# Attention and feed-forward on one core: the first step's v is loaded through ScalarE's DMA queue instead of SyncE's

## The chip, the cores and the metric

The kernel runs on one core of a Trainium2 chip. The metric is the device time of one execution in microseconds (us). Engines are named as in the profile: PE is TensorE (PEld its weight loads), DVE is VectorE, ACT is ScalarE, POOL is GpSimd, SP is SyncE. A DMA is issued by an instruction in the stream of an engine (here SP or ACT), which puts it into that engine's DMA queue; the bytes are moved by 16 DMA engines, which both queues share.

## What is computed

Sigmoid attention over 8 batches with 12 heads of 448 tokens and a head dimension of 64, and then a feed-forward layer with a squared ReLU over the 3584 tokens:

```python
scores = scale * np.matmul(q, k.transpose(0, 1, 3, 2)) - np.log(S)
attn = 1.0 / (1.0 + np.exp(-scores))
x = np.matmul(attn, v)            # then tokens x 768
h = x @ w_in
r = np.maximum(h, 0.0)
out = (s * (r * r) + b) @ w_out
```

The attention weights need no sum over the keys, so a block of scores can be used as soon as its sigmoid is there.

## The kernel before, in words

The attention part is a row of 24 steps, three for each of the 8 batches. One step works on four heads, as two pairs (index `i`); the two heads of a pair lie in the upper and the lower 64 partitions. A step's queries and keys stand in one tile `qk` (128 partitions, pair, queries or keys, 448 tokens: 896 KB), its values in a tile `v` (448 KB). After the 24 steps the feed-forward part runs to the end of the kernel (lines 556 to 1251); it isn't touched.

The fp32 products are made of three products of split numbers: a high part `qkh` and a low part `qkl` of queries and keys, and the products high by high, high by low and low by high (`PARTS`). For most steps ACT makes the high part and DVE the low part; for the first two steps DVE makes both, in pieces (`parts_dve`, lines 390 to 396, called in lines 594 and 601).

One step does this on PE: the scores of six key blocks of 128 tokens (`scores`, L420; the first two blocks of the first step use the unsplit numbers, L426, so that they needn't wait for a split), ACT's sigmoid on each block (L400), then the product with v (`attn_v`, L454, tile `pav`), and the remaining 64 keys of both pairs (`scores_last`, L441, and `attn_v_last`, L463). In the first step the products with v of the first pair come right behind its scores; the last keys' scores of this step follow, and then the second pair's products.

The order of the instructions on each engine is the order in which the program writes them. The tiles' semaphores are set by a framework; each engine works off its own list in order. A tile that several engines use is waited for by its readers.

The beginning of the program, around the change, is this:

- The first step's `qk` comes in five DMAs (`load` with `first=True`, lines 358 to 368): SP issues the first 128 keys of the first pair (L361), the rest of its keys (L363) and the second pair's keys (L365); ACT issues the first pair's queries (L362) and the second pair's queries (L364).
- `load_v` (lines 370 to 373) loads a step's v, and `load` without `first` the whole `qk` of a step in one DMA (L367); both are issued by SP.
- After these, ACT loads its table and computes a sigmoid into `e_bias` (L476), and DVE overwrites `e_bias` with a constant (L477). This stands ahead of DVE's first split.
- PE runs eight matmuls on constants (`WARM`, L482) before its first scores.
- SP then issues the first two pieces of the weights (L503, `st`), the second step's v and two small vectors (L549, L550).

DVE's first splits come in the order of line 594: the first pair's queries (448 columns), the second pair's queries, a block of the first pair's keys (128 columns), and the second pair's keys (384 columns).

```python
    loaded = {0: load(*quads[0], first=True)}
    load_v(*quads[0], loaded[0])
    loaded[1] = load(*quads[1])
    nc.scalar.activation(e_bias, nls, AF.Sigmoid)
    nc.vector.memset(e_bias, -896.0 * 2.0**23)
```

Of the kernel before, what the change touches and what calls it, by code (L numbers as in the profile page):

```python
# [94 lines left out]
def sigmoid_attention_relu2_ffn(  # L95
# [10 lines left out]
    nc = tc.nc  # L106
# [248 lines left out]
    quads = [(b, t) for b in range(B) for t in range(NQ)]  # L355
    NL = len(quads)

    def load(b, t, first=False):
        x = ld.tile([P, 2, 2, S], F32, tag="qk", name=f"qk_{b}_{t}")
        if first:  # L360
            nc.sync.dma_start(x[:, 0, 1, :P], qk[b, t][:, 0, 1, :P])  # L361
            nc.scalar.dma_start(x[:, 0, 0], qk[b, t][:, 0, 0])  # L362
            nc.sync.dma_start(x[:, 0, 1, P:], qk[b, t][:, 0, 1, P:])  # L363
            nc.scalar.dma_start(x[:, 1, 0], qk[b, t][:, 1, 0])  # L364
            nc.sync.dma_start(x[:, 1, 1], qk[b, t][:, 1, 1])  # L365
        else:
            nc.sync.dma_start(x, qk[b, t])  # L367
        return [x]

    def load_v(b, t, ld_):  # L370
        vt = ldv.tile([P, 7, 2, D], F32, tag="v", name=f"v_{b}_{t}")
        nc.sync.dma_start(vt, v[b, t])
        ld_.append(vt)

    NX = S + 3 * P
# [95 lines left out]
        nc.sync.dma_start(x_dram[b][:, 2 * t : 2 * t + 2], o)  # L471

    loaded = {0: load(*quads[0], first=True)}
    load_v(*quads[0], loaded[0])
    loaded[1] = load(*quads[1])
    nc.scalar.activation(e_bias, nls, AF.Sigmoid)  # L476
    nc.vector.memset(e_bias, -896.0 * 2.0**23)  # L477
# [68 lines left out]

    ticks(-1, "SP")
    load_v(*quads[1], loaded[1])
    nc.sync.dma_start(s_sb, s)  # L549
    nc.sync.dma_start(b_sb, b_)  # L550
# [44 lines left out]
    for n, (b, t) in enumerate(quads):  # L595
# [35 lines left out]
        if n + 2 < NL:  # L631
            load_v(*quads[n + 2], loaded[n + 2])
# [657 lines left out]
```

## Time and profile before

| | |
|---|---|
| time, median of 3 runs | 1038.63 us (1038.63 to 1038.81) |
| the profiled execution's own time | 1039.04 us |
| its span | 1037.2 us |
| PE busy | 1033.5 us (100% of the span) |
| DVE busy | 837.3 us (81%) |
| ACT busy | 617.0 us (59%) |
| DMA, mean over the span | 277 GB/s |
| granted TensorE clock | 1.00 |

The profile is of one execution. The page gives for each engine its busy time and share, and the chain of work that ended last, followed back from the last instruction. The timeline gives the start of an instruction, its length, the engine, the line, what it writes and reads, and in brackets how long the engine had been idle before it and what ended that. An engine's name with a q (SPq, ACTq) stands for the issue of a DMA or for a wait in its instruction stream; when the bytes have landed is given by the DMA view, as the time from the issue's start to the landing. Matmul ends are modelled, so the sum of PE's busy time isn't the time in which it works at its peak.

### The profile page before, as it was taken

What the parts mean: (1) busy time and instruction counts of PE and PEld (TensorE: products, weight loads), DVE (VectorE), ACT (ScalarE), POOL (GpSimd) and SP (SyncE); (2) the same over time, 40 slices, a digit from 0 to 9 for tenths busy, and PEclk for the clock granted to TensorE, in tenths of its full rate; (3) what the DMA queues carried; (4) which work ended last, traced back from release to release, by engine and by line L of the source; (5) the groups of instructions that cost most, each with busy time, mean ns of one, the idle gap of its engine ahead of it and who ended that gap; (6) DMA issues with size and microseconds to landing.
All of it is one profiled execution on the core that took longest, in us unless ns stands there. A gap on an engine that the chain in (4) does not pass through costs nothing.

```text
span 1037.2 us, 13906 instructions
## 1 busy us (share of the span) xinstructions
PE 1033.5 (100%) x5290; PEld 780.9 (75%) x5290; DVE 837.3 (81%) x910; ACT 617.0 (59%) x666; POOL 0.2 (0%) x4
## 2 busy tenths in 40 slices
PE   9999999999999999999999999999999999999998
PEld 4545555555888888888888888888888888888887
DVE  5999999995988965898898897796455789888777
ACT  7999999988776755564445344344445335552432
POOL 0000000000000000000000000000000000000000
PEclk9999999999999999999999999999999999999999
DMA  9788989994999999999686676897666666676773
GB/s 334 265 333 340 359 321 393 345 398 190 338 362 366 358 409 410 340 341 322 201 267 190 218 230 219 292 317 249 197 192 194 194 192 196 191 233 212 221 227 119
DMA packets 101569, 287.17 MB, mean 277 GB/s; under 512 B 10240, under 2 KB 20352, under 8 KB 101504
## 3 DMA queue, kind: packets, MB, share of 16 engines
q1 hardware_dynamic: 101216, 285.84, 79.3%
q8 instruction: 42, 0.69, 0.3%
q10 hardware_dynamic: 288, 0.46, 0.1%
q14 instruction: 23, 0.19, 0.0%
HBM read 198.18 MB, written 88.08 MB: 276 GB/s over the span
## 4 chain that ended last, share of the span: by engine, by line
PE 100%; DVE 0%; issue 0%
PE o L1225 31%; PE h L1095 31%; PE pav L454 11%; PE psc L420 9%; PE ph L563 6%; PE po L765 6%; PE psc_l L441 2%; PE pav L463 2%; PE idle L482 0%; PE psc L426 0%; DVE C_t L181 0%
## 5 line engine op out<-in xcount | busy, mean ns | idle before, releaser
L1095 PE MATMUL h<-s_0h,wu 128*128 128x512 f32 x480 | 148.0, 389 | 0.0
L1095 PE MATMUL h<-s_1h,wu 128*128 128x512 f32 x480 | 147.8, 389 | 0.0
L400 ACT ACTIVATE a<-psc,nls 128x896 f32<-128x896 f32 x144 | 132.7, 1008 | 12.9 <-PE psc L420 10.1
L454 PE MATMUL pav<-a,v 128*64 128x448 f32 x576 | 113.8, 543 | 0.0
L1095 PEld LDWEIGHTS h<-s_0h,wu 128*128 128x128 f32 x480 | 90.1, 188 | 18.8
L1095 PEld LDWEIGHTS h<-s_1h,wu 128*128 128x128 f32 x480 | 90.1, 188 | 18.6
L968 ACT COPY G<-h 128x1024 f32<-128x1024 f32 x48 | 48.8, 1017 | 85.4 <-PE h L1095 57.7
L860 ACT ACTIVATE G<-G,b_sb,s_sb 128x1024 f32<-128x1024 f32 x48 | 59.8, 1246 | 61.4 <-DVE G L857 60.7
L1095 PE MATMUL h<-s_0l,wu 128*128 128x512 f32 x240 | 93.4, 389 | 0.0
L1095 PE MATMUL h<-s_1l,wu 128*128 128x512 f32 x240 | 93.4, 389 | 0.0
L454 PEld LDWEIGHTS pav<-a,v 128*64 128x64 f32 x576 | 39.1, 137 | 63.8 <-issue 45.4
L178 DVE TENSOR_TENSOR G<-G,h 128x1024 f32<-128x1024 f32 x40 | 48.8, 1219 | 39.1 <-PE h L1095 38.9
L1225 PE MATMUL o<-g_3h,wu 128*128 128x512 f32 (+1 forms) x244 | 79.0, 385 | 0.0
L1225 PE MATMUL o<-g_1h,wu 128*128 128x512 f32 x240 | 78.8, 389 | 0.0
L1225 PE MATMUL o<-g_2h,wu 128*128 128x512 f32 x240 | 78.8, 389 | 0.0
L1225 PE MATMUL o<-g_0h,wu 128*128 128x512 f32 x240 | 78.8, 389 | 0.0
L765 PE MATMUL po<-g,w 128*128 128x512 f32 x288 | 67.7, 389 | 0.0
L765 PEld LDWEIGHTS po<-g,w 128*128 128x128 f32 x288 | 54.1, 188 | 11.2
L563 PE MATMUL ph<-x0h,w 128*128 128x512 f32 x192 | 61.7, 390 | 0.0
L420 PE MATMUL psc<-qkh 64*128 64x448 f32 x284 | 54.8, 382 | 0.0
L1225 PEld LDWEIGHTS o<-g_3h,wu 128*128 128x128 f32 x244 | 45.6, 188 | 9.2
L1225 PEld LDWEIGHTS o<-g_0h,wu 128*128 128x128 f32 x240 | 45.1, 188 | 9.4
(152 smaller groups left out, 2029.7 us busy)
## 6 DMA issues: line engine op xcount, KB each, us to landing
wu<-wd SPq DMA_DIRECT2D x240, 512.0 KB, 3.8
wd<-t SPq DMA_DIRECT2D x36, 768.0 KB, 8.1
qk<-qk_t SPq DMA_DIRECT2D x23, 896.0 KB, 7.1
st<-w_out SPq DMA_DIRECT2D x16, 768.0 KB, 9.3
st<-w_in SPq DMA_DIRECT2D x16, 768.0 KB, 9.2
wd<-w SPq DMA_DIRECT2D x16, 768.0 KB, 5.9
v<-v_t SPq DMA_DIRECT2D x24, 448.0 KB, 5.4
xd<-xo SPq DMA_DIRECT2D x24, 448.0 KB, 4.4
```

The source lines that it names most:

```text
L178: nc.vector.tensor_tensor(o, x, y, op=ALU.add)
L400: nc.scalar.activation(a, psc[:, :, :S], AF.Sigmoid, bias=nls, scale=SCALE)
L420: nc.tensor.matmul(o[:, j, :S], two[wi][r, i, cols], two[xi][r, i, :S], start=m == 0, stop=m == 2,)
L441: nc.tensor.matmul(psc[half[i], j, :S], x[r, i, 1, 3 * P :], x[r, i, 0, :], start=True, stop=True,)
L454: nc.tensor.matmul(pav[r, i, :S], ld_[1][:, 3 * i + c, j, :], a[i, c][:, j, :], start=c == 0, stop=False,)
L463: nc.tensor.matmul(pav[r, i, :S], ld_[1][half[i], 6, j, :], a[half[i], j, :], start=False, stop=True,)
L563: nc.tensor.matmul(ph, w[:, k, wi, kc * P : (kc + 1) * P], x0[h][xi][:, cc, :], start=m == 0, stop=m == 3 * NCC - 1,)
L765: nc.tensor.matmul(pos[e], w[:, k, wi, kc * P : (kc + 1) * P], g[:, gi, :], start=first and i == 0, stop=last and i == 2,)
L860: nc.scalar.activation(x, x, AF.Identity, bias=b_sb, scale=s_sb)
L968: nc.scalar.copy(g(m, h), bk)
L1095: nc.tensor.matmul(bk[:, j], wt[:, j, wi, c * P : (c + 1) * P], opd[i][xi][:, c, :], start=i == ch[0] and m == 0, stop=m == 3 * KC - 1, sk ...
L1225: nc.tensor.matmul(o, wt[:, f, wi, e * P : (e + 1) * P], g[gi][:, f, tk], start=(end or i == ch[0] and p == 0) and f == 0 and m == 0, stop ...
```

## The change

The first step's v is issued by ACT, after the second pair's queries, and no longer by SP, between the second pair's keys and the second step's `qk`. All other loads of v are issued by SP as before.

```diff
-    def load_v(b, t, ld_):
+    def load_v(b, t, ld_, queue=None):
         vt = ldv.tile([P, 7, 2, D], F32, tag="v", name=f"v_{b}_{t}")
-        nc.sync.dma_start(vt, v[b, t])
+        (queue or nc.sync).dma_start(vt, v[b, t])
         ld_.append(vt)
...
     loaded = {0: load(*quads[0], first=True)}
-    load_v(*quads[0], loaded[0])
+    load_v(*quads[0], loaded[0], nc.scalar)
     loaded[1] = load(*quads[1])
```

On ACT, at the start of the program (`qk_0_154` is the first step's tile of queries and keys, `v_0_160` its values), the difference is:

```order
 L362 DMA qk_0_154<-qk_t 128x448
 L364 DMA qk_0_154<-qk_t 128x448
+L372 DMA v_0_160<-v_t 128x896
 L476 ACT_TABLE_LOAD
 L476 ACTIVATE e_bias<-nls 128x1 [waits DVE_49]
```

One DMA has come in, ahead of the table load and the activation.

On SP, at the same place (`qk_1_162` is the second step's tile of queries and keys, `st_0_175` the first piece of the weights), it is:

```order
 L363 DMA qk_0_154<-qk_t 128x320
 L365 DMA qk_0_154<-qk_t 128x448
-L372 DMA v_0_160<-v_t 128x896
 L367 DMA qk_1_162<-qk_t 128x1792
 L503 DMA st_0_175<-w_out 128x768
```

The same DMA has gone, and the second step's queries and keys follow the second pair's keys directly. The rows that follow on SP are the same as before; the second piece of the weights, next but one, waits for the semaphore of the first pair's queries. On PE, DVE and POOL no instruction has moved and no wait has changed.

## Prediction

> **What bounds the kernel now.** I read the page first: the busy shares and the chain of work that ended last.
>
> ```profile
> span 1037.2 us, 13906 instructions
> PE 1033.5 (100%) x5290; PEld 780.9 (75%) x5290; DVE 837.3 (81%) x910; ACT 617.0 (59%) x666; POOL 0.2 (0%) x4
> PE 100%; DVE 0%; issue 0%
> ```
>
> TensorE (PE) is busy for 1033.5 of 1037.2 us and the chain consists of its work alone. A load can therefore move the time only by opening or closing a hole in PE. The change touches the first microseconds, so I read the chain there next, with the window 0 to 26 us (columns: start, length, what).
>
> ```profile
> 0.77 3.15 PE idle L482 x8
> 3.92 2.98 PE psc L426 x8
> 6.90 2.43 PE psc L420 x24
> 9.33 2.41 PE pav L454 x12
> 11.74 0.91 PE psc_l L441 x8
> ```
>
> The pieces join without a gap: 0.77 + 3.15 = 3.92, 3.92 + 2.98 = 6.90, and so on. PE begins with eight warm-up matmuls (L482), and from then on nothing is waited for. So the kernel before has nothing that an earlier v could give back: v is needed by pav (L454), at about 9.3, and pav follows on the heels of the scores. What can happen is that some load now comes later than PE has room for. So the working is a list of loads, each with its landing and the time at which PE would notice.
>
> The landings come from the DMA view, one window for each issue (KB each, us from issue to landing). In this order they are: the first pair's queries, the second pair's queries, the second pair's keys, the first step's v, and the next step's queries and keys.
>
> ```profile
> qk<-qk_t ACTq DMA_DIRECT2D x1, 224.0 KB, 2.8
> ...
> qk<-qk_t ACTq DMA_DIRECT2D x1, 224.0 KB, 3.6
> qk<-qk_t SPq DMA_DIRECT2D x1, 224.0 KB, 4.1
> ...
> v<-v_t SPq DMA_DIRECT2D x1, 448.0 KB, 5.3
> ...
> qk<-qk_t SPq DMA_DIRECT2D x1, 896.0 KB, 7.1
> ```
>
> Their issue times, and all who use the data, stand in the timeline:
>
> ```profile
> 0.72 0.41 ACTq L362 DMA_DIRECT2D qk<-qk_t  x1
> 1.16 0.45 ACTq L364 DMA_DIRECT2D qk<-qk_t  x1
> 1.64 0.42 SPq L365 DMA_DIRECT2D qk<-qk_t  x1
> 1.65 1.28 ACT L476 ACT_TABLE_LOAD   x1 [1.65 <-PEq L1280]
> 2.10 0.43 SPq L372 DMA_DIRECT2D v<-v_t  x1
> 2.58 0.43 SPq L367 DMA_DIRECT2D qk<-qk_t  x1
> 2.94 0.20 ACT L476 ACTIVATE e_bias<-nls 128x1 f32<-128x1 f32 x1
> 3.05 1.12 SPq L503 DMA_DIRECT2D st<-w_out  x2
> 3.21 0.06 DVE L477 MEMSET e_bias<- 128x1 f32 x1 [2.35 <-ACT e_bias L476]
> 3.58 0.40 DVE L394 CAST qkh<-qk 128x448 fp32r<-128x448 f32 x1 [0.32 <-DMA qk<-qk_t]
> 4.82 0.40 DVE L394 CAST qkh<-qk 128x448 fp32r<-128x448 f32 x1 [0.18 <-DMA qk<-qk_t]
> 5.76 1.01 ACT L400 ACTIVATE a<-psc,nls 128x896 f32<-128x896 f32 x1 [2.62 <-PE psc L426]
> 6.25 0.35 DVE L394 CAST qkh<-qk 128x384 fp32r<-128x384 f32 x1
> 6.64 0.56 DVE L181 TENSOR_TENSOR qkl<-qk,qkh 128x384 fp32r<-128x384 f32 x1
> 7.14 0.19 PEld L420 LDWEIGHTS psc<-qkh 64*128 64x128 f32 x2
> 7.54 0.20 PEld L420 LDWEIGHTS psc<-qkh,qkl 64*128 64x128 f32 x2
> 9.26 0.20 PEld L454 LDWEIGHTS pav<-a,v 128*64 128x64 f32 x4 [0.31 <-issue]
> 9.77 0.59 DVE L394 CAST qkh<-qk 128x832 fp32r<-128x832 f32 x1 [2.58 <-DMA qk<-qk_t]
> 11.96 1.03 DVE L181 TENSOR_TENSOR qkl<-qk,qkh 128x832 fp32r<-128x832 f32 x1
> 14.99 0.98 PE L441 MATMUL psc_l<-qk 64*64 64x448 f32 x8
> 16.65 0.47 PE L420 MATMUL psc<-qkh 64*128 64x448 f32 x2
> ```
>
> Issue plus delay gives the landings: second queries 1.16 + 3.6 = 4.76, second keys 1.64 + 4.1 = 5.74, v 2.10 + 5.3 = 7.40, next step's pair of tensors 2.58 + 7.1 = 9.68.
>
> **The change, part by part.**
>
> *One issue less on SyncE (SP).* SP loses an issue of 0.43 us (0.48 to the next one), and the next step's queries and keys go out at 2.10 instead of 2.58. At best they land 0.48 earlier, at 9.2. VectorE (DVE) waited 2.58 us for them before 9.77 and would end their split about half a microsecond sooner than 11.96 + 1.03 = 12.99. PE first touches this tensor at 14.99 and its split parts at 16.65, so there were already 2.0 us or more of room: worth 0. The later SP issues keep their places, because the second weight piece behind them waits for the landing of the first queries (0.72 + 2.8 = 3.52), which nothing here moves.
>
> *One issue more on ScalarE (ACT).* The issue stands between the second queries and the table load, and takes about what it took on SP, 0.43 us (ACT's own two took 0.41 and 0.45), with some 0.04 between neighbours: 0.47. The table load moves from 1.65 to 2.12 and the activation on e_bias from 2.94 to 3.41, ending at 3.61. Behind it waits DVE's memset of e_bias (L477), and behind that, in DVE's order, the whole first split. The memset moves from 3.21 to 3.68, so the first cast starts at about 3.75 instead of 3.58: 0.17 late. DVE then sat idle for 0.18 us before the cast at 4.82, waiting for the second queries. This hides the 0.17, with next to nothing left over; 0 on the path. If the cover were gone the 0.17 would reach the keys' split, where there is 0.34 more (next paragraph). ACT's own next work, the sigmoid at 5.76, had been preceded by 2.62 us of idling: 0.
>
> *The bytes of v in another queue.* This is the open term. Before, the second keys and v shared SP's queue, keys first, v behind them. Now v stands behind the second queries in ACT's queue and is not held behind the keys: from the moment that the second queries have been sent, somewhat before they land at 4.76, v's packets mix with the keys' packets. The keys can land later. I take the room for this from the rows: DVE reached the second keys at 6.25, 6.25 - 5.74 = 0.51 after they landed. Their low part was ready at 6.64 + 0.56 = 7.20, and PE loaded it as weights at 7.54: another 0.34. (The high part, ready at 6.25 + 0.35 = 6.60 and loaded at 7.14, has 0.54.) So the keys may land up to 0.51 + 0.34 = 0.85 later, at 6.59, before PE stops; each further microsecond is a microsecond of the kernel, since PE has no later slack.
>
> How late will they be? One bound is no delay, 5.74. The other is that keys and v change places entirely, and the keys land where v landed, at 7.40: 7.40 - 6.59 = 0.81 us lost. What lies between depends on how fast bytes flow while both are under way, and the windows of half a microsecond show a dip just there (last columns: DMA share, GB/s):
>
> ```profile
> 4.00:4.50 0.50, 0.50 (x2) 0.35 (x4) 0.49 (x1) 0.00 (x0) 0.00 (x0) 1.00 1.01 382
> 4.50:5.00 0.50, 0.50 (x4) 0.24 (x2) 0.32 (x2) 0.00 (x0) 0.00 (x0) 1.00 1.68 283
> 5.00:5.50 0.50, 0.50 (x2) 0.10 (x2) 0.47 (x2) 0.00 (x0) 0.00 (x0) 1.00 0.51 179
> ```
>
> From 4.5 to 5.5 the rate averages 231 GB/s, against 382 just before; the engines are taken all the same (a share of 1.68 and 0.51, about 1.1 on average). Long packets begin there, at the point where v's turn comes. If v's first packets are slow by themselves, they will now be slow in front of keys that have not been sent. The earlier sharing of the two queues is seen from 3.4 to 3.7:
>
> ```profile
> q10 hardware_dynamic: 39, 0.07, 60.1%
> q1 hardware_dynamic: 39, 0.04, 41.3%
> ```
>
> Both queues sent 39 packets in that time: they are served packet by packet in turn. [...]
>
> With even turns the keys' 224 KB share the engines with 224 KB of v or, v's packets being twice as large (3.5 KB for a partition against 1.75 KB), with up to 448 KB of it. At 382 GB/s that adds 224/382 = 0.6 to 448/382 = 1.2 us to a full overlap; if a third of the keys is through before it begins (they are issued 0.48 after the second queries, and land 0.98 after them), it is 0.4 to 0.8 us: the keys land at 6.1 to 6.5, just inside 6.59. I take 0.1 us for this term, near the lower end, and keep 0 and 0.81 as its bounds.
>
> *v itself.* It is needed by the first pav, 9.26, and landed at 7.40: 1.86 us of room. It is issued 0.48 earlier (about 1.62), and starts about when it started before, now sharing with the keys and then with the next step's tensor. I count 0; its lateness is the rival below.
>
> Sum: 0 + 0 + 0.1 + 0 = 0.1 us. The profiled execution took 1039.04 us, 1.84 more than its span; it becomes 1039.1. The median of the runs shown is 1038.63, 0.41 below the profiled one, so I forecast 1038.7.
>
> **Rivals.**
>
> *The keys are passed by v* (the upper bound). PE waits at the second pair's scores, at about 7.54, for up to 0.81 us. For it speaks the dip after 4.5; against it the equal packet counts. Time: 1038.63 + 0.3 to 0.8, so 1038.9 to 1039.4.
>
> *v comes too late, and the kernel is slower.* The place is the first pav (9.26). In SP's queue the next step's tensor goes out in packets of 7 KB for a partition, twice v's, and those of the weight pieces behind it are nearly as large, so v may get a third of the rate or less. The deciding point is a landing after 9.26. If v finishes only together with the next step's tensor, at 9.68, PE loses 9.68 - 9.26 = 0.42. If ACT's queue were starved until the weight pieces behind that tensor had landed too, it would be much more: their two issues end at 3.05 + 1.12 = 4.17, the second begins about 0.6 before that, and it landed 9.7 later,
>
> ```profile
> st<-w_out SPq DMA_DIRECT2D x1, 768.0 KB, 9.7
> ```
>
> so at about 13.3, and PE would lose 13.3 - 9.26 = 4.0 us, the kernel taking 1042.7. Over 0.2% (2.1 us) needs a landing of v after 11.3. Against it stand the equal counts of packets above: ACT's queue was not starved.
>
> *Nothing at all moves* (the change does not do what it says for the queues: bytes flow through the same sixteen engines, v lands where it did). Then 1038.63, as good as the forecast. A gain would need a hole in PE to close, and the chain shows none after 0.77; I allow 0.1 us for scatter.
>
> **How the numbers follow.** About 0.2% (2 us) is what a measurement of this kernel can tell from no change. Chances: the forecast, with the keys late but inside or nearly inside the room (nothing moving included), 0.62; keys passed by v, 0.28; v too late 0.07, of which 0.04 for more than 2.1 us; a gain of whatever kind 0.03, of which 0.01 over 0.2%. The likeliest is 1038.7. The range reaches from 1038.2 (0.4 below the median, about the distance between the runs shown and the profiled one, the other way) to 1039.5 (the upper bound of the keys, 1039.4, and 0.1 of scatter). Faster by over 0.2%: 0.01; slower by over 0.2%: 0.04; within: 0.95.
>
> **What would show it.** After the change the chain must still be PE alone, with warm-ups, raw scores, split scores and pav joined without gaps; pav's first piece at 9.33, or up to 0.8 later if the keys are passed. The table load should start near 2.12, the memset of e_bias near 3.7, the first cast near 3.75, and the cast at 4.82 should stay. The second keys should land at 6.1 to 6.5, and the cast at 6.25 start on time or wait for a DMA; v should land between 7 and 9, and the next step's tensor between 9.2 and 9.7. The forecast is wrong if the first pav waits for v, if PE's weight loads at 7.1 to 7.6 wait long for DVE, or if the time differs by more than 1 us while this first stretch has not moved.

## The result, and the profile after

| | before | after |
|---|---|---|
| median of 19 runs | 1038.89 us | 1040.72 us |
| lowest and highest | 1038.62 to 1039.5 | 1038.64 to 1043.21 |
| ratio, 95% interval | | 1.0018 (1.0012 to 1.0024) |
| profiled execution, its span | 1039.04, 1037.2 | 1040.07, 1038.1 |

The change costs 1.83 us, or 0.18%. It also makes the kernel scatter: 0.9 us lay between the extremes before, 4.6 us lie between them now, and the best execution after is as fast as the best before. The profiled execution is one of the milder ones, 1.03 us over the profiled one of before. Its page has PE at the same busy time in a longer span, and the chain has a DMA in it that wasn't there:

```profile
span 1038.1 us, 13906 instructions
PE 1033.4 (100%) x5290; PEld 780.4 (75%) x5290; DVE 837.3 (81%) x910; ACT 616.9 (59%) x666; POOL 0.2 (0%) x4
PE 99%; DMA 1%; ACTq 0%; DVE 0%; issue 0%
```

The chain in the window 0 to 26 us of the kernel after shows which:

```profile
1.18 0.45 ACTq L364
1.62 0.03 issue
1.66 8.23 DMA v<-v_t
9.88 0.14 issue
10.02 2.48 PE pav L454 x12
12.49 0.91 PE psc_l L441 x8
```

pav begins at 10.02 where it began at 9.33, and behind it everything follows without a gap as before. The start of the kernel is now bound by v itself, which lands at 9.88. In the timeline after, the instructions that answer to those of before are these:

```profile
1.66 0.45 ACTq L372 DMA_DIRECT2D v<-v_t  x1
2.11 0.43 SPq L367 DMA_DIRECT2D qk<-qk_t  x1
2.14 1.28 ACT L476 ACT_TABLE_LOAD   x1 [2.14 <-issue]
3.70 0.06 DVE L477 MEMSET e_bias<- 128x1 f32 x1 [2.84 <-ACT e_bias L476]
3.71 0.39 DVE L394 CAST qkh<-qk 128x448 fp32r<-128x448 f32 x1
4.68 0.39 DVE L394 CAST qkh<-qk 128x448 fp32r<-128x448 f32 x1
6.92 0.36 DVE L394 CAST qkh<-qk 128x384 fp32r<-128x384 f32 x1 [0.73 <-DMA qk<-qk_t]
7.43 0.47 PE L420 MATMUL psc<-qkh 64*128 64x448 f32 x2 [0.52 <-DVE qkh L394]
10.02 2.48 PE L454 MATMUL pav<-a,v 128*64 128x448 f32 x12 [0.39 <-DMA v<-v_t]
```

There are two holes in PE. At 7.43 it waits 0.52 us for the high part of the second pair's keys, which DVE could only begin at 6.92 because the keys landed late; at 10.02 it waits 0.39 us for v. The holes sum to 0.91. The matmuls before the first hole ran a little earlier than before (the eight of L426 took 2.46 us in the timeline instead of 3.06), so pav's start moves by less, 0.69 in the chain (9.33 to 10.02), and the span ends 0.9 later. The DMA view of the same execution (v, second keys) gives the delays:

```profile
v<-v_t ACTq DMA_DIRECT2D x1, 448.0 KB, 8.2
qk<-qk_t SPq DMA_DIRECT2D x1, 224.0 KB, 5.3
```

v takes 8.2 us instead of 5.3, though it was issued 0.44 earlier; the keys take 5.3 instead of 4.1 and land at 1.64 + 5.3 = 6.94 (6.90 by the report of their last engine). What v's bytes do is seen by the packets of ACT's queue (q10) in three windows, 4.5 to 6.5, 6.5 to 8 and 8 to 9.2 (packets, MB, share of the engines):

```profile
q10 hardware_dynamic: 119, 0.38, 50.7%
...
q10 hardware_dynamic: 14, 0.05, 7.6%
...
q10 hardware_dynamic: 7, 0.02, 3.7%
```

Most of v is through by 6.5. What comes later is a handful of packets, and they set the landing. The trace has sixteen reports of v's landing, read here as one from each of the 16 DMA engines for its own share; their times are:

```
v after:   5.99 6.01 6.07 6.17 6.38 6.39 6.43 6.45 6.46 6.47 6.49 6.63 6.87 8.46 9.29 9.88
v before:  6.20 6.25 6.29 6.39 6.49 6.60 6.66 6.83 6.84 6.99 7.04 7.08 7.28 7.34 7.39 7.45
```

Thirteen engines finished earlier than the latest of before, and three were up to 2.4 us later than that. On the late ones v's last packets stand about 0.41 us apart (7.12, 7.52, 7.92, 8.33, 8.73, 9.14): 140 ns for a packet of v and 272 ns, the length of one of the second step's 7 KB rows, between two of them. Before, in one queue, v's last engine (7.45) reported ahead of the first one of the second step's tensor (8.68). pav began only behind the last of the sixteen: at 10.02, 0.14 us after 9.88.

### The profile page after: what moved, and what is told of

Read it like the earlier page. It is cut to its first block, busy times and chain, and to the rows that moved or that the text cites. A ratio compares the mean times of both kernels' runs of the same rounds, so it can differ in the third digit from the quotient of the medians.

```text
span 1038.1 us, 13906 instructions
## 1 busy us (share of the span) xinstructions
PE 1033.4 (100%) x5290; PEld 780.4 (75%) x5290; DVE 837.3 (81%) x910; ACT 616.9 (59%) x666; POOL 0.2 (0%) x4
## 4 chain that ended last, share of the span: by engine, by line
PE 99%; DMA 1%; ACTq 0%; DVE 0%; issue 0%
PE o L1225 31%; PE h L1095 31%; PE pav L454 11%; PE psc L420 9%; PE ph L563 6%; PE po L765 6%; PE psc_l L441 2%; PE pav L463 2%; DMA v<-v_t 1%; ACTq L364 0%; DVE C_t L181 0%; ACTq L362 0%
## 5 line engine op out<-in xcount | busy, mean ns | idle before, releaser
L420 PE MATMUL psc<-qkh 64*128 64x448 f32 x284 | 54.7, 382 | 0.5 <-DVE qkh L394 0.5
L1225 PEld LDWEIGHTS o<-g_2h,wu 128*128 128x128 f32 x240 | 45.1, 188 | 9.4
```

What stands on the lines that cost most here:

```text
L420: nc.tensor.matmul(o[:, j, :S], two[wi][r, i, cols], two[xi][r, i, :S], start=m == 0, stop=m == 2,)
L1225: nc.tensor.matmul(o, wt[:, f, wi, e * P : (e + 1) * P], g[gi][:, f, tk], start=(end or i == ch[0] and p == 0) and f == 0 and m == 0, stop ...
```

## The experiments

Three theories were set against each other: that v takes turns with SP's loads, so that the last engines of v and of the keys come late ("turns"), that a load issued by ACT is slow by itself ("ACT queue"), and that the later table load and what hangs on it cost the time ("ACT shift"). "Before" in the results is the kernel before, run on the same chip: a median of 1038.82 us for e1 to e4, 1038.91 for f1 to f3 and g1, and a single run of 1039.56 for h1 to h3. The ratio is that to this median, with its 95% interval.

### SP's later loads held back (e1_hold)

The second step's load stands behind DVE's second piece of the first split; the column that DVE writes is overwritten by the load. For this the first step's splits are written earlier in the program.

```diff
+        if hold:
+            nc.vector.memset(x[:, 1, 1, S - 1 :], 0.0)
...
+    def next_load():
+        loaded[1] = load(*quads[1], hold=True)
```

> The kernel after the change, with all of SP's loads from the second step's queries and keys onward held back until DVE has split the second pair's queries (about 5.9 us; DVE writes one column of that tile first, so that the load has to wait for it). v stays on ACT. Theory 'turns' (v, no longer ahead of SP's loads, takes turns with them on every DMA engine): with nothing on SP behind the keys, v lands by 7.2 and pav does not wait for it; 1038.7 to 1039.4. Theory 'ACT queue' (a load issued by ACT is slow or late by itself): v lands at 8 to 11 as after the change, 1040 to 1041.5. Theory 'ACT shift' (the later table load and the later second keys cost the time): 1040 or more, with pav on time and the holes in the scores.

Measured: 1040.3 (1039.03 to 1040.99), ratio 1.0013 (1.0004 to 1.0022). The profiled execution was the fastest, with keys at 6.2, v at 6.8 and no hole; the median was far from it. So a loss is there without the later loads, which "turns" as I had put it did not say. Where it arises this profile doesn't show, hence two more executions.

### The same kernel in two more executions (h1_hold, h2_hold)

> The kernel of e1_hold (v on ACT, SP's later loads held) once more for its profile, since its first profile was its fastest execution (1039.03) while its median was 1040.3. 'Turns': in an execution over 1039.8 the second pair's keys, which share the engines with v alone, land at 7.4 or later, and the hole is at the second pair's scores; v lands by 7.5 and pav does not wait for it.

> As h1_hold, a second look. If an execution over 1039.8 has its keys by 6.7 and v by 8, the loss lies elsewhere, most likely behind the hold itself (the second step's tensor and the weights come some 4 us later), and e1_hold says nothing on the keys.

Measured: 1040.44 and 1040.52, 0.9 and 1.0 over the single run of before. The timeline of h1_hold, and below it that of h2_hold, at the second pair's keys:

```profile
7.54 0.36 DVE L396 CAST qkh<-qk 128x384 fp32r<-128x384 f32 x1 [1.37 <-DMA qk<-qk_t]
8.05 0.47 PE L424 MATMUL psc<-qkh 64*128 64x448 f32 x2 [1.03 <-DVE qkh L396]
```

```profile
7.78 0.36 DVE L396 CAST qkh<-qk 128x384 fp32r<-128x384 f32 x1 [1.62 <-DMA qk<-qk_t]
8.29 0.47 PE L424 MATMUL psc<-qkh 64*128 64x448 f32 x2 [1.52 <-DVE qkh L396]
```

The keys land at 7.52 and 7.76, v at 7.70 and 7.93, and pav waits for nothing. With v alone beside them the keys land up to two microseconds later than in the profile of before, and a hole of 1.0 and 1.5 us opens at the scores. The packets show the turns: in h2_hold the last packets of the keys begin at 6.39, 6.60, 6.81, 7.01 and 7.22, some 0.21 us apart, which is one packet of keys (74 ns) and one of v (140 ns). That is "turns", with the keys as its victim.

### v back on SP, the second step's tensor on ACT (e2_swap)

```diff
-    loaded[1] = load(*quads[1])
+    loaded[1] = load(*quads[1], queue=nc.scalar)
```

> The kernel before the change, with the second step's queries and keys issued by ACT in the place where the change puts v; v is on SP as before, directly behind the second pair's keys. 'Turns': v again takes turns, with the 896 KB now on ACT; it lands at 8 to 11, pav waits, 1039.3 to 1041.5. 'ACT queue': v is on SP and lands by 7.6; 1038.6 to 1039.2. 'ACT shift': ACT has one issue more, as after the change; 1040 or more with v on time.

Measured: 1041.66 (1041.12 to 1043.59), ratio 1.0029 (1.0017 to 1.0040), so at least as bad as the change, with v on SP (its median excess is larger, but the two intervals overlap). "ACT queue" is out: v is late (2.10 + 8.2 = 10.3) from SP's queue too. The place that I had named was wrong, since pav does not wait; the keys do the damage, 2.68 us in one hole:

```profile
9.10 0.36 DVE L394 CAST qkh<-qk 128x384 fp32r<-128x384 f32 x1 [2.85 <-DMA qk<-qk_t]
9.61 0.47 PE L420 MATMUL psc<-qkh 64*128 64x448 f32 x2 [2.68 <-DVE qkh L394]
```

Here the last packets of the keys begin at 6.71, 7.05, 7.39, 7.73, 8.06 and 8.40, some 0.34 us apart: one packet of keys (74 ns) and one 7 KB row (272 ns), as turns would have it.

### v strictly behind the second step's tensor, both on SP (e3_behind)

```diff
-    load_v(*quads[0], loaded[0])
     loaded[1] = load(*quads[1])
+    load_v(*quads[0], loaded[0])
```

> The kernel before the change with v and the second step's queries and keys exchanged in SP's own queue: v strictly behind all 896 KB. It gives the price of a late v without any sharing between queues. All theories: v lands at 9.6 to 10.1, pav waits 0.4 to 0.8 us, 1039.2 to 1039.8. 'Turns' says besides that this worst strict order costs less than the change (1040.72) and scatters less, since no engine can fall back to turns with the weight pieces.

Measured: 1040.12 (1039.74 to 1041.08), ratio 1.0013 (1.0005 to 1.0022); v landed at 10.15.

```profile
10.28 2.48 PE L454 MATMUL pav<-a,v 128*64 128x448 f32 x12 [1.16 <-DMA v<-v_t]
```

The hole is larger than I had said, 1.16 instead of 0.4 to 0.8, because the scores ended at 9.12 in this execution. The medians stand in the expected order, 1.30 us over before as against 1.83 for the change, but the intervals of the two ratios overlap, so that the strict order costs less is not shown. It scatters less: over 1.3 us in 11 runs, where the change has 4.6 in 19.

### The second step's tensor in four DMAs of short rows (e4_small)

```diff
+            for i in range(2):
+                for j in range(2):
+                    nc.sync.dma_start(x[:, i, j], qk[b, t][:, i, j])
```

> The kernel after the change with the second step's queries and keys loaded in four DMAs with rows of 1.75 KB in place of one with rows of 7 KB; v stays on ACT. 'Turns', packet for packet: a packet of v now waits for 74 ns of another instead of 272, v lands at 6.8 to 8.5, pav waits seldom, 1038.8 to 1039.7. If the engines share by bytes and not by packets, nothing changes: v at 8 to 11, 1040 to 1041.5. 'ACT queue' says the same as that.

Measured: 1040.93 (1040.29 to 1043.05), ratio 1.0020 (1.0011 to 1.0029). The expectation failed. The median is that of the change within the intervals: with rows a quarter as long the loss stays, so the length of the second step's rows alone does not make it. The profiled execution was the slowest of its kernel. In it v did come earlier, 1.65 + 7.0 = 8.65, and pav did not wait for it, but the keys landed at 8.41. Its hole is the first row, and the chain behind it the other two:

```profile
8.94 0.47 PE L424 MATMUL psc<-qkh 64*128 64x448 f32 x2 [2.08 <-DVE qkh L398]
```

```profile
8.94 2.60 PE psc L424 x18
11.54 3.60 PE pav L458 x12
```

The twelve pav matmuls take 3.60 us instead of 2.41, and the mean granted clock is 0.998. The trace has it at one half from 10.5 to 13.9 us (0.50 in the windows 11 to 12 and 12 to 13): after its idling of 2.08 us PE ran slower for a while, and the twelve pav matmuls took 1.19 us more, so here the loss was larger than the hole itself. More on this below.

### ACT's shift without the bytes (f2_act)

```diff
+    nc.scalar.dma_start(s_sb, s)
     load_v(*quads[0], loaded[0])
...
-    nc.sync.dma_start(s_sb, s)
```

> The kernel before the change with one more issue on ACT in the place where the change puts v, but of a load of 0.5 KB (the vector s, which SP issued later); v stays on SP. It shifts the table load and DVE's first cast as the change does, without the bytes. 'Turns': the shift is hidden, 1038.6 to 1039.2. 'ACT shift': most of the loss is there, 1040 or more.

Measured: 1039.31 (1039.03 to 1039.75), ratio 1.0003 (0.9994 to 1.0012), 0.4 over before and just above what "turns" allowed. "ACT shift" is out as the main cause; a few tenths of a microsecond are not excluded. In its profile DVE's first two casts start at 3.67 and 4.72 (before: 3.58 and 4.82). The profile also shows how far a landing varies with v on SP: the keys land at 6.66, 0.9 later than in the profile of before (in e3_behind at 6.40), and v at 8.57. PE has holes of 0.45 and 0.34 us at the scores, and pav still begins at 9.31 (before: 9.27 in the timeline), because PE's first matmuls ran faster (the eight of L426 took 1.77 us instead of 3.06).

### v on ACT, kept clear of both neighbours (f1_clean)

The first hold stands behind DVE's first cast, the second one behind its third.

```diff
+        if hold:
+            nc.vector.memset(vt[:, 6, 1, D - 1 :], 0.0)
         (queue or nc.sync).dma_start(vt, v[b, t])
...
+    def hold_v():
+        load_v(*quads[0], loaded[0], nc.scalar, hold=True)
...
+    def hold_next():
+        loaded[1] = load(*quads[1], hold=True)
```

> v is issued by ACT, but only once DVE has made its first cast (about 4.0 us, so that its bytes start when the second pair's keys are nearly through), and SP's loads from the second step's queries and keys onward are held back until DVE's third cast (about 6 us). So v is on ACT's queue and overlaps neither the keys nor the later loads for long; the table load is back at 1.65. 'Turns' (whatever is under way in the other queue makes the keys and v late): keys by 5.9, v by 8.3, no hole, 1038.5 to 1039.2, as before the change. 'ACT queue' (a load issued by ACT is slow by itself): v 5 us or more after its issue, past 9.3, 1039.8 or more.

Measured: 1039.29 (1038.81 to 1040.18), ratio 1.0004 (0.9995 to 1.0013). Delays of the second keys and of v, from the DMA view, and the first PE wait of the timeline behind the warm-up:

```profile
qk<-qk_t SPq DMA_DIRECT2D x1, 224.0 KB, 3.5
...
v<-v_t ACTq DMA_DIRECT2D x1, 448.0 KB, 3.3
```

```profile
18.11 0.47 PE L427 MATMUL psc<-qkh 64*128 64x448 f32 x2 [0.54 <-ACT a_l L407]
```

Nearly alone, a load from ACT's queue takes 3.3 us, the shortest that v took in any trace. The keys land at 5.15, and there is no hole before 18. The 0.54 there belongs to the hold: the second step's tensor and the weights come some 4 us later than before. The median is 0.4 over before, 0.1 above what I had allowed, and the interval includes no difference.

### v on ACT behind the keys, nothing held (f3_vlate, and h3_vlate for a second profile)

This is f1_clean without the second hold: v goes out at about 4.05, and SP's later loads follow the keys at once.

> v is issued by ACT once DVE has made its first cast (about 4.0 us), and SP is not held: the keys are nearly through when v starts, and v overlaps only the second step's queries and keys and the weights. It leaves the loss by v alone. 'Turns': keys by 6.0, v at 9 to 11, pav waits, 1039.3 to 1041.5, no hole in the scores. If the whole loss of the change came through the keys: v by 9.2 and 1038.6 to 1039.2.

> The kernel of f3_vlate once more: its median was 1044.13, its profile 1042.01 with a hole of 2.9 us at pav. 'Turns' with a slower clock after a long hole: in an execution near 1044 v lands at 12 to 13, the hole is over 3 us, and the matmuls behind it run longer (12 of pav over 3 us instead of 2.4), the granted clock below 1.000. Without that, the hole alone has to make the whole excess.

Measured: f3_vlate 1044.13 (1042.01 to 1044.71), ratio 1.0051 (1.0038 to 1.0065); h3_vlate 1045.21. This is far outside what I expected. The keys are on time (4.6 and 3.8 us after issue, landing at 6.24 and 5.44), and v alone is late, at 11.86 and 12.44. This is not turns from the start: v's queue sends its first packet only at 7.95 and 8.33, when SP's second-step tensor is nearly through (its engines report from 7.55 to 8.45, and from 7.19 to 9.03), and the weights then travel beside v. The two profiled executions, f3_vlate first (its hole is 2.53, not the 2.9 that the expectation of h3_vlate names):

```profile
11.99 2.48 PE L461 MATMUL pav<-a,v 128*64 128x448 f32 x12 [2.53 <-DMA v<-v_t]
```

```profile
12.58 4.75 PE L461 MATMUL pav<-a,v 128*64 128x448 f32 x12 [3.81 <-DMA v<-v_t]
```

In the second one pav's twelve matmuls take 4.75 us, about twice the usual 2.41, the mean granted clock is 0.997 (one half from 11.1 to 18.0 us), and the span is 1043.2. pav begins 3.3 us later than before (12.58 as against 9.27 in the timeline); after the slow matmuls the second pair's products begin 5.9 later (18.50 as against 12.58), and the span is 6.0 longer.

### The kernel after once more (g1_after)

> The kernel after the change once more, for a second profile of it, because its time scatters from 1038.64 to 1043.21. 'Turns': the time of this execution is explained by the landings in its own trace: the hole at the scores is the second keys' landing less 6.6, the hole at pav is v's landing less the time at which the scores end, and together they give the span's excess over 1036.8 to 1037.2; where PE stands idle for more than about 2 us its next matmuls run longer than in the other profiles.

Measured: 1039.92, span 1038.1. The same two late loads: keys at 6.86, v at 9.84 with two late engines (9.44 and 9.84; the third last came at 7.05).

```profile
6.88 0.36 DVE L394 CAST qkh<-qk 128x384 fp32r<-128x384 f32 x1 [0.72 <-DMA qk<-qk_t]
9.98 2.48 PE L454 MATMUL pav<-a,v 128*64 128x448 f32 x12 [0.40 <-DMA v<-v_t]
```

This time the scores show no hole of their own in PE's row: the first matmuls ran slower (2.99 us for the eight of L426, as against 2.46 in the other profile of this kernel), so PE came to the keys later. So the expectation, which would have had a hole at the scores as well, missed in that. pav starts 0.65 later than before (9.98 as against 9.33), and the span ends 0.9 later.

## Why the prediction was wrong

**What bounds the kernel, and that nothing could be gained:** right. PE's chain had no hole; the losses in the traces are holes in the first 13 us and slower matmuls behind them (and the hold's own hole in f1_clean), and no run of any variant was faster than the best of before on its chip. pav did begin earlier in two profiles (8.69 in f1_clean, 8.87 in e1_hold), but no time came out shorter for it.

**The issue less on SP:** right in its size (the second step's tensor went out at 2.11; the first weight piece, too, went out earlier, at 2.58 instead of 3.05). But I costed it at nothing because nobody needs that tensor before 14.99, and did not see that its bytes, no longer behind v, would compete with v. Here the load that nobody waited for was not free: with its bytes in turns with v's (one late packet of v every 0.41 us instead of 0.14) v landed at 9.88 instead of 7.40.

**The issue more on ACT:** right. The table load began at 2.14 (forecast 2.12) and the first cast at 3.71 (3.75). f2_act has the shift alone and finds no difference outside its interval.

**The bytes of v in another queue, counted as 0.1 us:** this is the first step that failed. The prediction put the keys "just inside 6.59", at 6.1 to 6.5, from mean rates, and took 7.40 for the latest. They landed at 6.90 and 6.86 in the two profiles of the kernel after, and where v was the only competitor at 6.2 in e1_hold and at 7.5 to 7.8 in h1_hold and h2_hold. The landing is the last of the sixteen reports, and a mean rate did not give the last: in the profiled execution after, fifteen engines had landed the keys by 6.02, the last at 6.90. Two things made it late. One is the turns: in h2_hold and e2_swap the slowest keys came one packet every 0.21 and 0.34 us (above), and in g1_after the last ones also stand 0.21 apart. The other is the long packets behind the dip at 4.5 to 5.5. Before, these are mostly v's own first packets (from 4.58 on, up to 1.17 us each), they stand behind the keys, and fifteen of sixteen engines had landed their keys by 5.24. In the profiled execution after, one of the few long ones is a packet of the keys themselves, 0.92 us from 5.16, directly after a packet of v that took 0.62 from 4.53; the keys' last seven packets follow from 6.07 to 6.50. That these belong to one engine is inferred from the times.

**v itself, counted as 0:** the second step that failed, and the rival named it. The place was right (the first pav), the partner was right (the 7 KB rows), and the landing that the rival worked out for its milder form, 9.68, lies near the 9.88 and 9.84 measured, and its 0.42 us near the 0.39 and 0.40 of the hole. That nearness is in part luck: 9.68 was the landing of the second step's tensor before the change, while after it v lands ahead of that tensor (10.12), and with short rows in e4_small the loss stays. I had put it at 0.07 because both queues had sent equal numbers of packets from 3.4 to 3.7, "ACT's queue was not starved" (four of SP's 39 were records of under 512 bytes). Equal turns were no evidence against it: the late packets of v came one every 0.41 us, v's own 140 ns and the 272 ns of one 7 KB row, which is what equal turns against longer packets give, instead of one every 0.14.

**The price of a microsecond:** counted one for one. That holds roughly in e2_swap and f3_vlate (holes of 2.68 and 2.53 us, spans 2.7 and 2.8 longer than in the profile of before), but not in e4_small and h3_vlate, where the matmuls behind the hole were slower (3.60 and 4.75 us for pav's twelve instead of 2.41), nor in f2_act, where two holes of 0.45 and 0.34 us did not delay pav (9.31 as against 9.27) because PE had been faster before them (1.77 us for the eight of L426 instead of 3.06). The room of 0.85 was itself read in an execution with slow first matmuls. Two of the 19 runs of the kernel after, 1042.58 and 1043.21, have a granted clock of 0.998 as e4_small has, which fits the same.

**The chances:** the two rivals together are what happened in the profiled executions: keys and v were late side by side. I had treated them as alternatives, the larger one as improbable, and the range ended where the first alone would end. Of the 2.0 us by which the time lies over the forecast, 0.26 is the base: the three runs shown had a median of 1038.63, the nineteen of the result 1038.89.

What stays open: the kernel after was traced in two executions below its median, 1040.07 and 1039.92, so how the 1.83 us divides between keys and v is not shown; in these two both loads are late. With v on SP the keys also came as late as 6.40 (e3_behind) and 6.66 (f2_act, with a load of 0.5 KB in ACT's queue), so a part of their lateness may be scatter. Why the packets pause, and why the keys came later in two of three executions of the held kernel (7.5 to 7.8) than in the kernel after (6.9), the runs don't tell.

## What to carry to other kernels

Here the queue was also an order: loads that are waited for soon stood ahead of the others in SP's queue, and before the change the engines reported the keys by 5.77, v from 6.20 to 7.45 and the second step's tensor from 8.68 to 9.65. Moving one of them to another queue gave up that protection for it and for its neighbour, while the DMA engines stayed the same (from 4.5 to 6.5 of the kernel after, ACT's queue took 50.7% of the sixteen and SP's 48.9%). The move saved 0.47 us of issue that nobody waited for, and cost 1.83. Before such a move, list what is in flight beside the moved load and how late the slowest engine may be, not the mean: here v's sixteen reports spread from 5.99 to 9.88.

## What the runs showed that was not expected

- In e2_swap one DMA engine in sixteen decided: fifteen had landed the keys by 7.22, the last at 9.08; PE waited 2.68 us.
- In f3_vlate a load waited for its first packet while a load that another engine had issued earlier went through. v was issued at 4.08, and its queue sent a single packet of it before 8.0 (at 7.95), while the second step's tensor, issued at 2.1 by SP, went through. The rows are those of ACT's queue in the windows 6.5 to 8 and 8 to 9.2:

```profile
q10 hardware_dynamic: 1, 0.00, 0.6%
...
q10 hardware_dynamic: 42, 0.15, 31.0%
```

 In f1_clean, with only the end of the keys in SP's queue, the first packet came 0.97 us after the issue. Why it waited is not shown.
- In the traces of before and of h1_hold the long packets mostly stand at the beginning of a load and not at a fixed time. Before, those over 0.65 us that begin between 4 and 11 us are all v's, from 4.58 to 4.90. In h1_hold they are the first packets of the second step's tensor, which is held there and starts at 6.69: 0.78 to 1.14 us for the first six, where 272 ns is usual.
- PE's first matmuls ran slower than the later ones (in the profile of before L420's first pair took 0.78 us at 6.32, and its next eleven 0.37 or 0.38), and the moment at which this ended differed between executions, even of one kernel. The eight matmuls of L426 took 3.06 us in the profile of before, 2.46 and 2.99 in the two of the kernel after and 1.77 in f2_act; the trace's record of the granted clock begins at 6.47, 5.26, 6.33 and 3.57 us there. A hole near the start has to be read together with this.
- A hole in PE of 3.81 us was followed by matmuls of about double length (4.75 us for twelve instead of 2.41); one of 2.08 us by a smaller slowdown (3.60), and one of 2.53 by none (2.48). The clock was one half from 10.51 to 13.92 in e4_small (3.41 us) and from 11.14 to 17.97 in h3_vlate (6.83 us). In h3_vlate it fell inside the hole, some 2.4 us after the last matmul had ended; in e4_small it fell 1.57 us after the hole of 2.08 us had ended at 8.94. What lowers the clock, and for how long, the runs don't tell.
